# Decode attention from 64 KiB rows: four heads in a tile, three slots, K transposed in place

## The chip, the cores and the metric

The kernel runs on one core of one Trainium2 chip. The metric is the device time in microseconds (us) of one execution, the median of several.

## The reference

One decode step: layer norm, attention over a cache of 8192 keys for 4 sequences and 32 heads, and a gated feed-forward part (FFN), added to x.

```python
q = (xn @ wq).reshape(4, 1, 32, 128).transpose(0, 2, 1, 3)
scores = einsum("bhqd,bhkd->bhqk", q, k_cache) * 128 ** -0.5   # k_cache: 4 x 32 x 8192 x 128, bf16
o = einsum("bhqk,bhkd->bhqd", softmax(scores), v_cache)
return x + o.reshape(4, 1, 4096) @ wo + (silu(xn @ w_gate) * (xn @ w_up)) @ w_down
```

K and V are 268 MB each, and every byte is read once. That makes this a kernel of transfers: 551 MB in all.

## The kernel before

A tile is one sequence and HT = 2 heads of K or of V: 4 MiB, 32 KiB of contiguous memory for each of the 128 partitions (64 partitions a head, 128 keys each). Five slots of 32 KiB per partition hold what is loaded. VectorE turns K in blocks of 32 x 32 (r = QB = 32 in the access pattern), piece by piece into buffers of its own; TensorE makes scores from these; P V of tile i - 2 follows.

```python
HT = 2; T = HT * Sk // P          # 128 keys a partition
SLOT = T * Dh; NSLOT = 5; LP = 2
slots = tc.tile_pool(name="slots", bufs=NSLOT)
kt_pool = tc.tile_pool(name="ktp", bufs=5)
def load_k(n):
    j, b = divmod(n, B)
    t_ = slot()
    nc.sync.dma_start(out=t_[:], in_=A_k_cache[b, j * HT:(j + 1) * HT, :, :]
                      .rearrange("h (p t) d -> (h p) (t d)", t=T))
def t_piece(n, g):                # 16 keys of every partition
    kt = kt_pool.tile([P, w], dt.bfloat16, name="kt")
    nc.vector.transpose(out=kt[:]..., in_=k_tiles[n][:, g * w:(g + 1) * w]...)
for i in range(NT + LP):
    load_k(i + 2); load_v(i)
    for g in range(NTG):
        t_piece(i, g); s_piece(i, g)        # transpose, then 4 score matmuls
    # ... maximum and exponentials of two tiles at once, P V of tile i - 2 ...
```

Of the kernel before, what the change touches and what calls it, by code (L numbers as in the profile page):

```python
# [8 lines left out]
dt = mybir.dt  # L9
# [6 lines left out]
def kernel(  # L16
# [20 lines left out]
    assert D % P == 0 and F % P == 0 and Sk == 64 * P and H % 4 == 0  # L37
# [3 lines left out]
    HT = 2  # L41
# [8 lines left out]
    NSLOT = 5  # L50
    LP = 2
# [13 lines left out]
    kt_pool = ctx.enter_context(tc.tile_pool(name="ktp", bufs=5))  # L65
    pp = ctx.enter_context(tc.tile_pool(name="pp", bufs=2))
# [18 lines left out]
    x_sb = persist.tile([B, D], dt.bfloat16, name="x_sb")  # L85
    nc.scalar.dma_start(out=x_sb[:], in_=x_flat[:, :])
    wq_t = slot()
    nc.sync.dma_start(out=wq_t[:], in_=A_wq.rearrange("(p c) n -> p (c n)", c=EC))
# [9 lines left out]
    def load_v(n, parts=(T,)):  # L98
        j, b = divmod(n, B)
        t_ = slot()  # L100
        src = A_v_cache[b, j * HT:(j + 1) * HT, :, :].rearrange("h (p t) d -> (h p) (t d)", t=T)
        c0 = 0
        for w in parts:
            c1 = c0 + w * Dh
            nc.sync.dma_start(out=t_[:, c0:c1], in_=src[:, c0:c1])
            c0 = c1
        v_tiles[n] = t_
# [5 lines left out]
    ident = const.tile([P, P], dt.bfloat16, name="ident")  # L113
    make_identity(nc, ident[:])
# [4 lines left out]
    zq = [const.tile([P, 2, 4, ZW], dt.bfloat16, name=f"zq{i}") for i in range(2)]  # L119
    for z_ in zq:  # L120
        nc.gpsimd.memset(z_[:], 0.0)
# [8 lines left out]
    def by_row(ap):  # L130
        return ap.rearrange("p (y a b g r) -> p y b a g r", y=HT, a=2, b=2, r=2)[:, :, :, :, :, 0]

    rowb = const.tile([P, HT, 2], dt.float32, name="rowb")
    nc.vector.reduce_sum(out=rowb[:], in_=by_row(ident_f[:]), axis=AX.XY)
    rowb_q = const.tile([P, HT, 2], dt.float32, name="rowb_q")
# [12 lines left out]
    xf = persist.tile([B, D], dt.float32, name="xf")  # L148
    nc.vector.tensor_copy(out=xf[:], in_=x_sb[:])
    xsum = persist.tile([B, 1], dt.float32, name="xsum")  # L150
    nc.vector.reduce_sum(out=xsum[:], in_=xf[:], axis=AX.X)
    mean = persist.tile([B, 1], dt.float32, name="mean")
    nc.vector.tensor_scalar(out=mean[:], in0=xsum[:], scalar1=1.0 / D, scalar2=None, op0=ALU.mult)
    xc = kt_pool.tile([B, D], dt.float32, name="kt")
    nc.vector.tensor_scalar(out=xc[:], in0=xf[:], scalar1=mean[:, 0:1], scalar2=None, op0=ALU.subtract)
    sq = kt_pool.tile([B, D], dt.float32, name="kt")
    nc.vector.tensor_tensor(out=sq[:], in0=xc[:], in1=xc[:], op=ALU.mult)
    vsum = persist.tile([B, 1], dt.float32, name="vsum")
    nc.vector.reduce_sum(out=vsum[:], in_=sq[:], axis=AX.X)
# [4 lines left out]
    xn_bf = kt_pool.tile([B, D], dt.bfloat16, name="kt")  # L164
    nc.vector.tensor_scalar(out=xn_bf[:], in0=xc[:], scalar1=rstd[:, 0:1], scalar2=None, op0=ALU.mult)  # L165
# [16 lines left out]
    q_bf = slots.tile([P, NH, 2, 8, NQ, QB], dt.bfloat16, name="slot")  # L182
# [10 lines left out]
    pick = ident[:].rearrange("p (c x) -> p c x", c=NQ)[:, :, 0:B]  # L193
# [8 lines left out]
    yfx = persist.tile([B, D], dt.float32, name="yfx")  # L202
    otn = persist.tile([P, H, B], dt.bfloat16, name="otn")

    DH = D // 2
    yo_ps = [psY.tile([B, DH], dt.float32, name="yo_ps") for _ in range(2)]
    ffn = {}

    def load_ffn():
        wgu_t, wd_t = slot(), slot()  # L210
        w = EC * F
        nc.sync.dma_start(out=wgu_t[:, 0:w], in_=B_w_gate.rearrange("(p c) f -> p (c f)", c=EC))
        nc.sync.dma_start(out=wgu_t[:, w:2 * w], in_=B_w_up.rearrange("(p c) f -> p (c f)", c=EC))
        nc.sync.dma_start(out=wd_t[:, 0:FC * D], in_=B_w_down.rearrange("(p c) e -> p (c e)", c=FC))
        ffn["w"] = (wgu_t[:, 0:w].rearrange("p (c f) -> p c f", c=EC),
                    wgu_t[:, w:2 * w].rearrange("p (c f) -> p c f", c=EC),
                    wd_t[:, 0:FC * D].rearrange("p (c e) -> p c e", c=FC))

    def do_ffn():
        wg, wu, wd = ffn["w"]  # L220

        gu_ps = psM.tile([P, 2, FC * B], dt.float32, name="mps")
        for i, w in enumerate((wg, wu)):
            for fc in range(FC):
                for c in range(EC):
                    mm(gu_ps[:, i, fc * B:(fc + 1) * B], w[:, c, fc:F:FC], xnt_w[:, c, 0:B],
                       start=(i == 0 and fc == 0 and c == 0))
        eg = persist.tile([P, FC * B], dt.float32, name="eg")
        nc.scalar.activation(out=eg[:], in_=gu_ps[:, 0, :], func=ACT.Exp, scale=-1.0)
        nc.vector.tensor_scalar(out=eg[:], in0=eg[:], scalar1=1.0, scalar2=None, op0=ALU.add)  # L230
        sig = persist.tile([P, FC * B], dt.float32, name="sig")
        nc.vector.reciprocal(out=sig[:], in_=eg[:])
        gs = persist.tile([P, FC * B], dt.float32, name="gs")
        nc.vector.tensor_tensor(out=gs[:], in0=gu_ps[:, 0, :], in1=sig[:], op=ALU.mult)
        ht = persist.tile([P, FC * B], dt.bfloat16, name="ht")
        nc.vector.tensor_tensor(out=ht[:], in0=gs[:], in1=gu_ps[:, 1, :], op=ALU.mult)
        yf_ps = psM.tile([B, D], dt.float32, name="mps")
        for fc in range(FC):
            mm(yf_ps[0:B, :], ht[:, fc * B:(fc + 1) * B], wd[:, fc, :], start=(fc == 0))
        nc.vector.tensor_tensor(out=yfx[:], in0=yf_ps[0:B, :], in1=xf[:], op=ALU.add)  # L240

        for j in range(2):
            mm(yo_ps[j][0:B, :], ident_f[0:B, 0:B], yfx[:, j * DH:(j + 1) * DH], start=True)
# [6 lines left out]
    def load_wo():  # L250
        t_ = slot()
# [8 lines left out]
    kts, s_ps, pt, nmx, osb, rcp = {}, {}, {}, {}, {}, {}  # L260
    rs_t = {}

    def build_q(gr):
        j, bp = divmod(gr, 2)
        for a in range(NQ):
            h = j * HT + a // 2
            half, cg, hh = h // 16, (h % 16) // 4, h % 4
            nc.vector.tensor_copy(  # L268
                out=zq[gr % 2][a * QB:(a + 1) * QB, :, :, XO + a * QB].rearrange("p b (j r) -> p r j b", r=2),
                in_=qt[a * QB:(a + 1) * QB, half, :, hh * 2:hh * 2 + 2, cg * B + bp * 2:cg * B + bp * 2 + 2])  # L270

    def t_piece(n, g):

        w = TG * Dh
        kt = kt_pool.tile([P, w], dt.bfloat16, name="kt")
        src = k_tiles[n][:, g * w:(g + 1) * w].bitcast(dt.uint32)
        nc.vector.transpose(out=kt[:].bitcast(dt.uint32).rearrange("p (j t r) -> p t j r", j=2, r=QB),  # L277
                            in_=src.rearrange("p (t j r) -> p t j r", j=2, r=QB))
        kts[n, g] = kt

    def s_piece(n, g):
        gr, bb = divmod(n, 2)
        if bb == 0 and g == 0:
            s_ps[gr] = psS.tile([P, 512], dt.float32, name="sps")
        kt = kts.pop((n, g))[:].rearrange("p (j n r) -> p j n r", j=2, r=2)
        off = XO - 2 * (bb * NTG + g)
        for jp in range(4):
            mm(s_ps[gr][:], zq[gr % 2][:, bb, jp, off:off + P], kt[:, jp // 2, :, jp % 2],
               start=(bb == 0 and g == 0 and jp == 0))

    def max_1(gr):
        mx = small.tile([P, 1], dt.float32, name="mx")
        nc.vector.reduce_max(out=mx[:], in_=s_ps[gr][:], axis=AX.X)  # L293
        nmx[gr] = mx

    def max_2(gr):

        mps = psM.tile([P, 512], dt.float32, name="mps")
        nc.tensor.matmul(mps[:, 0:P], lhsT=nmx.pop(gr)[:, 0:1].to_broadcast([P, P]), rhs=ident_f[:, :],  # L299
                         is_transpose=True, start=True, stop=True, skip_group_check=True)  # L300
        nm = small.tile([P, HT, 2], dt.float32, name="nm")
        nc.vector.tensor_reduce(out=nm[:], in_=by_row(mps[:, 0:P]), axis=AX.XY, op=ALU.max, negate=True)  # L302
        nc.vector.tensor_tensor(out=nm[:], in0=nm[:], in1=rowb_q[:], op=ALU.mult)
        nb = small.tile([P, 1], dt.float32, name="nb")
        nc.vector.reduce_sum(out=nb[:], in_=nm[:], axis=AX.XY)
        p_ = pp.tile([P, 512], dt.bfloat16, name="p_")
        rs = small.tile([P, 1], dt.float32, name="rs")
        nc.scalar.activation(out=p_[:], in_=s_ps.pop(gr)[:], func=ACT.Exp, bias=nb[:, 0:1], scale=qscale,
                             accum_out=rs[:])
        pt[gr] = p_  # L310
        rs_t[gr] = (rs, mps)

    def pt_turn(gr):
        p_ = pt[gr]
        t_ = ptz[gr % 2]
        HP = P // HT
        for y in range(HT):
            nc.vector.transpose(out=t_[y * HP:(y + 1) * HP, :, y, :, :].rearrange("p s u x -> p s (u x)"),  # L318
                                in_=p_[y * HP:(y + 1) * HP, :].rearrange("p (s w) -> p s w", s=4))
        pt[gr] = t_[:].rearrange("p s y u x -> p (s y u x)")  # L320

    def row_sums(gr):
        j, bp = divmod(gr, 2)
        rs, mps = rs_t.pop(gr)
        mm(mps[:, P:P + B], rs[:, 0:1].to_broadcast([P, P]), rowb[:].rearrange("p y b -> p (y b)"), start=True)
        if bp == 0:
            rcp[j] = small.tile([P, HT, B], dt.float32, name="rcp")
        nc.vector.reciprocal(out=rcp[j][:, :, 2 * bp:2 * bp + 2],  # L328
                             in_=mps[:, P:P + B].rearrange("p (y b) -> p y b", y=HT))

    def p_off(n, k):
        g, s = divmod(k, TG // NV)
        return s * HT * NV * QB + 2 * ((n % 2) * NTG + g)

    def pv_chunk(n, k):
        j, b = divmod(n, B)
        w = HT * NV
        off = p_off(n, k)
# [151 lines left out]
```

## Time and profile before

| | before |
|---|---|
| time, median of 3 | 1288.92 us (1288.82 to 1288.93) |
| DMA main queue, share of 16 engines' span | 99.4% |
| DMA packets | 21529, 551.49 MB |
| PE / VectorE busy | 84% / 57% |
| instructions | 11189 |

Read the transfers first. When 16 engines are full from the first to the last slice, the busy shares of PE and VectorE say only how much room they have. The lines are in the prediction below. A "packet" is one record of a DMA transfer in the trace. Here that is one partition's row: the trace has 16256 packets of 32 KiB, as many as 127 tiles of 128 rows.

### The profile page before, as it was taken

What the parts mean: (1) busy time and instruction counts of PE and PEld (TensorE: products, weight loads), DVE (VectorE), ACT (ScalarE), POOL (GpSimd) and SP (SyncE); (2) the same over time, 40 slices, a digit from 0 to 9 for tenths busy, and PEclk for the clock granted to TensorE, in tenths of its full rate; (3) what the DMA queues carried; (4) which work ended last, traced back from release to release, by engine and by line L of the source; (5) the groups of instructions that cost most, each with busy time, mean ns of one, the idle gap of its engine ahead of it and who ended that gap; (6) DMA issues with size and microseconds to landing.
All of it is one profiled execution on the core that took longest, in us unless ns stands there. A gap on an engine that the chain in (4) does not pass through costs nothing.

```text
span 1287.1 us, 11189 instructions
## 1 busy us (share of the span) xinstructions
PE 1083.1 (84%) x4778; PEld 430.3 (33%) x4778; DVE 738.1 (57%) x951; ACT 39.7 (3%) x87; POOL 5.3 (0%) x13
## 2 busy tenths in 40 slices
PE   4888888888888798897997888888887988978788
PEld 1334333333333333332333333333333333333334
DVE  6663556546556556466556566465465465573544
ACT  1000000000000000000000000000000000000000
POOL 1000000000000000000000000000000000000000
PEclk9898898998989999898998989989899898989899
DMA  9999999999999999999999999999999999999997
GB/s 407 427 430 435 437 425 437 429 436 431 432 435 428 436 432 433 431 432 435 431 435 428 434 432 431 436 431 433 430 434 431 437 430 432 433 431 427 433 434 304
DMA packets 21529, 551.49 MB, mean 428 GB/s; under 512 B 2268, under 2 KB 2792, under 8 KB 3944
## 3 DMA queue, kind: packets, MB, share of 16 engines
q1 hardware_dynamic: 21464, 550.78, 99.4%
q8 instruction: 37, 0.61, 0.2%
q14 instruction: 12, 0.10, 0.0%
q10 hardware_dynamic: 16, 0.01, 0.0%
HBM read 550.77 MB, written 0.00 MB: 428 GB/s over the span
## 4 chain that ended last, share of the span: by engine, by line
DMA 50%; PE 31%; DVE 14%; issue 5%; ACT 1%; SPq 0%; DVEq 0%
DMA slot<-in_A_k_cache_dram 44%; PE oacc L76 17%; PE sps L76 12%; DVE kt L277 11%; DMA slot<-in_A_v_cache_dram 6%; PE mps L76 1%; DVE ptz L318 1%; DVE o L356 1%; PE xps L76 1%; DVE o_sb L354 1%; ACT o_sb L353 0%; PE mps L299 0%; DVE otn L377 0%; PE yo_ps L76 0%; DVE rcp L328 0%
## 5 line engine op out<-in xcount | busy, mean ns | idle before, releaser
L76 PE MATMUL sps<-kt,zq 128*128 128x512 bf16 x2048 | 578.3, 421 | 145.2 <-DVE kt L277 128.7
L277 DVE STREAM_TRANSPOSE kt<-slot 128x1024 uint32<-128x1024 uint32 x512 | 587.6, 1210 | 90.4 <-DMA slot<-in_A_k_cache_dram 89.5
L76 PE MATMUL oacc<-slot,ptz 128*8 128x512 bf16 x2016 | 450.4, 379 | 0.4 <-DMA slot<-in_A_v_cache_dram 0.4
L76 PEld LDWEIGHTS <-zq 128*128 128x128 bf16 x2048 | 212.0, 104 | 496.1 <-issue 317.0
L76 PEld LDWEIGHTS <-ptz 128*8 128x8 bf16 x2016 | 177.5, 92 | 258.1 <-issue 27.8
L328 DVE RECIPROCAL rcp<-mps 128x4 f32<-128x4 f32 x32 | 5.9, 183 | 281.9 <-PE mps L76 281.9
L354 DVE TENSOR_TENSOR o_sb<-o_sb,rowu 128x512 f32<-128x512 f32 x16 | 11.1, 693 | 89.2 <-ACT o_sb L353 89.0
L76 PE MATMUL xps<-rowy,o 128*32 128x4 f32 (+1 forms) x228 | 13.5, 205 | 37.3 <-DVE o L356 37.3
L293 DVE TENSOR_REDUCE mx<-sps 128x1 f32<-128x512 f32 x32 | 22.1, 692 | 18.5 <-PE sps L76 18.5
L76 PEld LDWEIGHTS xps<-rowy,o 128*32 128x32 f32 (+1 forms) x228 | 12.1, 154 | 44.9 <-DVE o L356 44.9
L268 DVE COPY zq<-qt 32x8 bf16<-32x8 bf16 x128 | 21.3, 166 | 1.3
L302 DVE TENSOR_REDUCE nm<-mps 128x4 f32<-128x64 f32 x32 | 7.2, 225 | 24.0 <-PE mps L299 24.0
L356 DVE TENSOR_REDUCE o<-o_sb 128x128 f32<-128x512 f32 x16 | 16.3, 1020 | 0.5
L76 PEld LDWEIGHTS mps<-rowb,rs 128*128 128x128 f32 x64 | 9.5, 186 | 13.8 <-issue 13.8
L76 PEld LDWEIGHTS <-slot 128*128 128x128 bf16 x272 | 11.7, 126 | 3.5 <-DVE slot L188 2.6
L76 PE MATMUL mps<-rowb,rs 128*128 128x4 f32 x64 | 12.3, 263 | 0.0
L353 ACT COPY o_sb<-oacc 128x512 f32<-128x512 f32 x16 | 9.4, 586 | 76.8 <-PE oacc L76 76.8
L377 DVE TENSOR_TENSOR otn<-xps,rcp 32x16 bf16<-32x16 f32 x28 | 4.8, 170 | 11.7 <-PE xps L76 10.3
L299 PE MATMUL mps<-ident_f,mx 128*128 128x128 f32 x32 | 10.3, 323 | 0.8 <-DVE mx L293 0.8
L299 PEld LDWEIGHTS mps<-ident_f,mx 128*128 128x128 f32 x32 | 4.3, 133 | 14.7 <-DVE mx L293 14.2
L170 PE MATMUL xps<-ident,kt 4*128 4x4 bf16 x4 | 0.3, 173 | 10.1 <-DVE kt L165 10.1
L76 PE MATMUL yo_ps<-slot,otn 128*4 128x256 bf16 x64 | 8.2, 281 | 0.3 <-DVE otn L366 0.3
(150 smaller groups left out, 148.5 us busy)
## 6 DMA issues: line engine op xcount, KB each, us to landing
slot<-in_A_k_cache_dram SPq DMA_DIRECT2D x64, 4096.0 KB, 39.2
slot<-in_A_v_cache_dram SPq DMA_DIRECT2D x62, 4096.0 KB, 36.8
slot<-in_A_v_cache_dram SPq DMA_DIRECT2D x7, 1024.0 KB, 22.3
slot<-in_A_wq_dram SPq DMA_DIRECT2D x1, 4096.0 KB, 12.3
slot<-in_A_wo_dram SPq DMA_DIRECT2D x1, 3584.0 KB, 40.2
slot<-in_B_w_gate_dram SPq DMA_DIRECT2D x1, 1792.0 KB, 31.9
slot<-in_B_w_up_dram SPq DMA_DIRECT2D x1, 1792.0 KB, 35.8
slot<-in_B_w_down_dram SPq DMA_DIRECT2D x1, 1792.0 KB, 30.9
```

The costliest lines, as they stand in the source:

```text
L76: nc.tensor.matmul(out_ap, lhsT=lhsT, rhs=rhs, start=start, stop=True, skip_group_check=True, **kw)
L268: nc.vector.tensor_copy(out=zq[gr % 2][a * QB:(a + 1) * QB, :, :, XO + a * QB].rearrange("p b (j r) -> p r j b", r=2), in_=qt[a * QB:(a + ...
L277: nc.vector.transpose(out=kt[:].bitcast(dt.uint32).rearrange("p (j t r) -> p t j r", j=2, r=QB), in_=src.rearrange("p (t j r) -> p t j r", ...
L293: nc.vector.reduce_max(out=mx[:], in_=s_ps[gr][:], axis=AX.X)
L299: nc.tensor.matmul(mps[:, 0:P], lhsT=nmx.pop(gr)[:, 0:1].to_broadcast([P, P]), rhs=ident_f[:, :], is_transpose=True, start=True, stop=True ...
L302: nc.vector.tensor_reduce(out=nm[:], in_=by_row(mps[:, 0:P]), axis=AX.XY, op=ALU.max, negate=True)
L318: nc.vector.transpose(out=t_[y * HP:(y + 1) * HP, :, y, :, :].rearrange("p s u x -> p s (u x)"), in_=p_[y * HP:(y + 1) * HP, :].rearrange( ...
L328: nc.vector.reciprocal(out=rcp[j][:, :, 2 * bp:2 * bp + 2], in_=mps[:, P:P + B].rearrange("p (y b) -> p y b", y=HT))
L353: nc.scalar.copy(out=o_sb[:].rearrange("p u d -> p (u d)"), in_=o_acc[j % 2][:])
L354: nc.vector.tensor_tensor(out=o_sb[:], in0=o_sb[:], in1=rowu[:].unsqueeze(2).to_broadcast([P, NV, Dh]), op=ALU.mult)
L356: nc.vector.reduce_sum(out=o1[:], in_=o_sb[:].rearrange("p u d -> p d u"), axis=AX.X)
L377: nc.vector.tensor_tensor(out=otn[q0:q1, blk * 4:blk * 4 + 4, :], in0=xps[q0:q1], in1=r_[q0:q1, y, :].unsqueeze(1).to_broadcast([QB, 4, B] ...
```

## The change

The intent is longer rows, so fewer packets. With HT = 4 a tile is 8 MiB and a row 64 KiB. The kernel keeps three such slots (192 KiB a partition, for 160 KiB in five before) and little else of size beside them: K is transposed in place in its slot, V(i) is loaded into the slot that K(i) has left, small things of the start lie beside wq, and P V of a tile is cut into halves that lie on both sides of the next tile's scores.

```diff
-    HT = 2
+    HT = 4
-    NSLOT = 5
-    LP = 2
+    NSLOT = 3
-    kt_pool = ctx.enter_context(tc.tile_pool(name="ktp", bufs=5))
-    def t_piece(n, g):
-        kt = kt_pool.tile([P, w], dt.bfloat16, name="kt")
-        nc.vector.transpose(out=kt[:]..., in_=src...)
+    def turn_k(n, parts):
+        t0 = 0
+        for w in parts:
+            t1 = t0 + w * TG
+            ap = k_tiles[n][:, t0 * Dh:t1 * Dh].bitcast(dt.uint32)
+            nc.vector.transpose(out=ap, in_=ap)
+            t0 = t1
+    for i in range(NT - 1):
+        turn_k(i, (2,) * 8 if i < 2 else (4, 4, 2, 2, 2, 2))
+        if i >= 3:
+            pv_to(i - 2, NK)            # second half of P V(i - 2)
+            load_k(i + 1)
+        for g in range(NTG):
+            score(i, g)
+        ...  load_v(i)                  # into the slot of K(i)
+        max_1(i)
+        pv_to(i - 1, 8); max_2(i); pt_turn(i)
+        pv_to(i - 1, NK // 2)           # first half of P V(i - 1)
+        row_sums(i)
+    # the last tile: wo with half of V, the other half in pieces of 48, 32, 24, 16 and 8 keys
```

(Cut: the end, the FFN in one slot with its sum straight into the output's PSUM, the finish of a group of heads in PSUM without ScalarE's copy.)

## The prediction

> **What bounds the kernel now.** I read the page from the top. The first view is the span in slices and the DMA totals.
>
> ```profile
> span 1287.1 us, 11189 instructions
> PE 1083.1 (84%) x4778; PEld 430.3 (33%) x4778; DVE 738.1 (57%) x951; ACT 39.7 (3%) x87; POOL 5.3 (0%) x13
> DMA  9999999999999999999999999999999999999997
> GB/s 407 427 430 435 437 425 437 429 436 431 432 435 428 436 432 433 431 432 435 431 435 428 434 432 431 436 431 433 430 434 431 437 430 432 433 431 427 433 434 304
> DMA packets 21529, 551.49 MB, mean 428 GB/s; under 512 B 2268, under 2 KB 2792, under 8 KB 3944
> q1 hardware_dynamic: 21464, 550.78, 99.4%
> ```
>
> The 16 DMA engines are busy in every slice but the last, and the main queue alone fills 99.4% of the span. PE at 84% and VectorE (DVE) at 57% have room. The windows view says how the edges differ from the middle; its last two columns are the DMA share and GB/s.
>
> ```profile
> 0.00:2.00 2.00, 0.00 (x0) 0.00 (x0) 1.03 (x4) 0.67 (x1) 1.33 (x9) 1.00 0.64 166
> 640.00:960.00 320.00, 272.29 (x1140) 106.20 (x1137) 189.69 (x241) 8.57 (x20) 0.00 (x0) 0.94 1.00 432
> 1270.00:1280.00 10.00, 10.00 (x108) 5.24 (x106) 1.40 (x3) 0.59 (x1) 0.00 (x0) 1.00 0.78 327
> 1280.00:1287.00 7.00, 3.35 (x74) 2.42 (x70) 1.09 (x3) 0.36 (x1) 0.00 (x0) 0.59 0.11 44
> ```
>
> So the time is: about 1.8 us of start, a transfer that never pauses, and a tail. Last comes the chain at the end, in order of time (start, length, what):
>
> ```profile
> 1265.54 17.13 DMA slot<-in_A_v_cache_dram
> 1282.67 0.05 issue
> 1282.71 0.60 PE xps L76 x16
> 1283.32 0.03 issue
> 1283.34 0.18 DVE otn L366
> 1283.52 0.04 issue
> 1283.56 1.03 PE yo_ps L76 x4
> 1284.59 0.02 issue
> 1284.61 0.36 ACT res L458
> ```
>
> The last piece of V lands at 1282.7, and 4.4 us of work and output follow. The page's chain of waits puts only 50% on DMA, which would mislead: it steps through what released each DMA issue, though another transfer was still moving at that moment. The slices decide.
>
> I then took the trace's records of single DMA packets. In the median a packet of 1024, 4096, 8192, 14336 and 32768 B takes 46, 159, 309, 535 and 1213 ns. The slope from 4096 to 32768 B is 1054 ns per 28672 B, 36.76 ns per 1000 B or 27.2 GB/s an engine; what is left over is 1213 - 1204.6 = 8.4 ns a packet, whatever its size. A 4-byte packet (a completion) takes 9 ns. All packet times sum to 1281.5 us for each of 16 engines. At nearly every moment 16 data packets are in flight; only from about 1275 on are there 9, for some 4 us, as seven engines have finished first.
>
> [...] 432 GB/s in the middle, 27.2 x 16 = 435 from the slope. [...] the trace shows 8.4, so I use 8.4.[...] eight pieces of 1024 uint32 took 9.11 us, 1.14 us each, so about 1.11 ns an element with its start.
>
> **The change, part by part.**
>
> *Longer rows.* HT = 4 makes a K or V tile 8 MiB with 64 KiB per partition. Before, 127 tiles (wq, 64 K, 62 V) of 128 rows give 16256 packets of 32 KiB; that is the count in the trace. After, 32 K and 30 V tiles give 62 x 128 = 7936 rows of 64 KiB. If each is one packet, it should take 65536 B x 36.76 = 2409.4, plus 8.4, so 2418 ns against 2 x 1213 = 2426. Work per engine: 7936 x 2418 / 16 = 1199.3 us; wq 128 x 1213 / 16 = 9.7; the 31st V in four parts of 16 KiB rows, 512 x 611 / 16 = 19.6; the last V's first half 256 x 611 / 16 = 9.8; its pieces of 48, 32, 24, 16 and 8 keys, 128 x (460 + 309 + 234 + 159 + 84) / 16 = 10.0; wo 8.9 + 1.5; FFN weights 384 x 535 / 16 = 12.8; instruction fetches as before, 37 x 929 / 16 = 2.1. Completions: some 81 transfers for 141, x 16 x 9 ns / 16 = 0.7 for 1.3. Sum 1274.4. The same sum for before, with its median packet times, is 1279.3, and the records have 1281.5 as some packets are slower; so add 2.2: **1276.6 against 1281.5, a gain of 4.9 us**. The bytes themselves do not change.
>
> *Three slots instead of five.* This is the risk: does a transfer ever have to wait for a slot? An 8 MiB tile takes 8.39 MB / 0.432 = 19.4 us, so a round (one K, one V) is 38.8 us. Let K(i) land at 0. V(i-1) then moves until 19.4, K(i+1) until 38.8, and V(i) must be ready to issue by 38.8 into K(i)'s own slot. VectorE turns K(i) from 0: 16384 elements a partition in six instructions, at 1.14 us per 1024 at most (18.2 us). PE first does the second half of P V(i-2), 32 x 0.22 = 7 us (the trace: 32 in 7.08), which frees the slot for K(i+1) at about 1 to 8, due at 19.4: 11 us or more in hand. The scores follow the transposes and end some 2.5 us after the last, at about 21; V(i) is due at 38.8: **18 us in hand**. PE per round: 64 scores paced by VectorE (18 to 20 us), 64 P V x 0.22 = 14.2, small things about 1: some 34 of 38.8. VectorE per round: 18.2, maximum and its three small ones 1.3, four turns of P about 2.5, row sums, q and the finish about 1.5: 24 of 38.8. Neither becomes the bound.
>
> *The start.* wq lands at 12.3, K0 about 32, K1 about 51. V0 goes into wq's slot, free near 20, due at 51. The FFN weights go into K0's slot after scores 0 (32 + 18 + 3 = 53, due at 70); K2 into K1's slot after scores 1 (near 77, due at 83, the tightest); V1 after all of P V(0) (near 93, due at 102); K3 after the FFN (near 104, due at 121). Estimates, each with 6 us or more.
>
> *The end.* K31, V30, wo with half of V31, then the other half into K31's slot: scores 31 end some 20 us after K31 lands, and V30 and the wo load (38 us) run meanwhile. After the last landing come 8 small matmuls for 16 (0.3 for 0.6 us), the same scaling (0.2), four heads x 4 matmuls of 128 columns for two heads x 2 of 256 (about 1.2 for 1.0), and the output. The tail stays near 4.4 us; sum of this part 0.
>
> *In place on VectorE, ScalarE's copy dropped.* 512 transposes become about 200[...], all beside the transfers: worth 0.
>
> Sum: 1288.9 - 4.9 = **1284.0 us**.
>
> **Rivals.**
> 1. *A wait for a slot takes the place of what is won.* For it: three slots, K(i) and V(i) sharing one, and a load of 8 MiB lands only as a whole. Against it: 18 us in hand. If transposing in place were half as slow again (27 us), scores would end at 30, still in time; twice as slow (36), they would end at 38.8, and each round loses a few us: 31 rounds x 2 us = 60, or 1345. A wait in the start alone costs 5 to 10 us: 1290 to 1294.
> 2. *A 64 KiB row goes as two packets of 32 KiB.* Nothing in this trace tells. Then only the completions are saved: 1288.
> 3. *HBM dislikes the 64 KiB pitch.*[...] A loss of 1 to 3% would make 1297 to 1325.
> 4. *A gain over 2%* needs 1263 us[...].
>
> **Range and chances.** The centre is 1284, with rival 2 (about one in four) at 1288, so 1279 to 1293 should hold it 8 times in 10. Under 1279 only if the slower packets of before go too. Faster by over 2%: 0.01. Slower by over 2% (over 1314.7), from rival 1 or 3 in full: 0.05. Within 2%: 0.94.
>
> **What would show it.** Right: a DMA line of nines with 432 to 436 GB/s throughout, some 13,000 packets in all, the 64 KiB packets at about 2418 ns, their sum near 1277, DMA issues of V(i) well before the transfer ahead ends, and an end like that of before. Two packets a row: 21,000 packets again. Wrong by rival 1: slices under 425 GB/s in the middle, and K landing later than 38.8 us after the last. Wrong by rival 3: engines busy all through at a lower GB/s, packets over 2418. The mean of a transpose should be near 2.3 us for 2048 elements; over 4 us would mean that in place is slow.

The places marked as cut in the prediction held figures and reasons that no trace or run of this case shows. Rival 3 stays as a possibility that had not been measured, with an assumed loss; against rival 4, the trace's slope gives an estimate: 551.5 MB at 27.2 x 16 = 435 GB/s take 1267 us, more than the 1263 it needs. Times of the kernel after with "about" or "some" are estimates from the trace of the kernel before. One of them is the 1.2 us for 16 matmuls of 128 columns at the end: the trace of the kernel before has 16 of 256 columns in 1.91 us, and 1.03 was measured after. That an 8 MiB load is of use only as a whole (rival 1) is how the kernel after ran: while K(i+1) was moving, from 668 to 687.0 us, VectorE stood idle for its last 10.8 us.

## The result

The changed kernel took **1285.91 us** (median of 4, 1285.87 to 1285.94) against 1288.87 us for the kernel before in the same session: 2.96 us less. The ratio is 0.9977 with an interval of 0.9962 to 0.9992. The forecast was 1284.0 and 4.9 us less, range 1279 to 1293.

The page of the kernel after, its span, engines, DMA and queue lines:

```profile
span 1284.1 us, 11309 instructions
PE 1003.1 (78%) x5170; PEld 460.9 (36%) x5170; DVE 736.5 (57%) x621; ACT 30.1 (2%) x71; POOL 5.9 (0%) x12
DMA  9999999999999999999999999999999999999997
GB/s 425 423 432 430 443 429 431 432 437 427 438 437 431 433 431 441 427 425 448 431 425 444 434 423 439 439 425 433 439 431 429 435 433 438 429 433 442 427 414 313
DMA packets 12600, 551.49 MB, mean 429 GB/s; under 512 B 1277, under 2 KB 1801, under 8 KB 3081
q1 hardware_dynamic: 12536, 550.77, 99.2%
```

The line of nines is the same as before, the bytes are the same, and the packets have gone from 21529 to 12600. A row of 64 KiB did go as one packet: the trace has 7936 of 65536 B. (Single slices now swing between 414 and 448 GB/s, so the prediction's sign "432 to 436 throughout" does not hold slice by slice, and some slices in the middle lie under its warning mark of 425. The time did not follow, and the windows view below is level. The swing goes with the size of the packets: slices 2 to 38 lie between 423 and 448 here, between 425 and 437 with 32 KiB rows, before, and between 429 and 432 with 16 KiB rows, in a_quarter below.) The windows view of the kernel after, as in the prediction (busy by engine, PE clock, DMA share, GB/s):

```profile
640.00:960.00 320.00, 253.72 (x1134) 112.81 (x1133) 181.72 (x149) 6.22 (x16) 0.00 (x0) 0.90 1.00 434
1270.00:1280.00 10.00, 6.29 (x194) 5.85 (x192) 0.00 (x0) 0.00 (x0) 0.00 (x0) 0.50 0.58 239
```

In the middle 434 GB/s stand against 432 before, and the end is of the same kind. The chain of waits at the end of the kernel after (start, length, what):

```profile
1255.84 23.23 DMA slot<-in_A_v_cache_dram
1279.07 0.05 issue
1279.11 0.59 PE xps L74 x16
1279.70 0.03 issue
1279.73 0.39 PE xps L74 x8
1280.12 0.02 issue
1280.15 0.18 DVE otn L380
1280.33 0.04 issue
1280.38 1.03 PE yo_ps L74 x16
1281.41 0.02 issue
1281.43 0.26 ACT res L486
```

V's second last piece lands at 1279.1 and its last about 0.6 us later, against 1282.7 before, and the rest takes as long as it did, 4.4 us. So the gain lies before the last landing, in the stream of transfers.

How the three slots behave shows in the timeline of VectorE in one round (start, length, what, in brackets the idle time before it):

```profile
648.39 17.54 DVE L298 STREAM_TRANSPOSE slot<-slot 128x4096 uint32<-128x4096 uint32 x6 [10.50 <-DMA slot<-in_A_k_cache_dram]
668.32 0.69 DVE L311 TENSOR_REDUCE mx<-sps 128x1 f32<-128x512 f32 x1 [2.39 <-PE sps L74]
...
671.95 2.85 DVE L335 STREAM_TRANSPOSE ptz<-p__3063 32x512 bf16<-32x512 bf16 x4 [0.93 <-ACT p__3063 L326]
676.02 0.18 DVE L345 RECIPROCAL rcp<-mps 128x4 f32<-128x4 f32 x1 [1.22 <-PE mps L74]
686.98 4.45 DVE L298 STREAM_TRANSPOSE slot<-slot 128x4096 uint32<-128x4096 uint32 x1 [10.77 <-DMA slot<-in_A_k_cache_dram]
```

K lands at 648.4 and the next K at 687.0, 38.6 us apart, the time that two tiles of 8.39 MB take at 434 GB/s. VectorE is done with everything by 676.2 and waits for K: it is the transfers that set the round. In the same round K(i+1) was issued at 644.7 and V(i) at 668.3 (the timeline of all engines):

```profile
644.72 0.33 SPq L104 DMA_DIRECT2D slot<-in_A_k_cache_dram  x1
668.31 0.33 SPq L117 DMA_DIRECT2D slot<-in_A_v_cache_dram  x1
```

**Where the 3 us are.** I took the records of single packets of both traces. The 64 KiB packet takes 2418 ns, as forecast. All packet times sum to 1277.1 us an engine, on average over the 16, against 1281.5: 4.5 us less, close to the forecast 4.9. But the last landing came only 3.0 us earlier. The length of a packet is not the distance to the next one: the commonest distance from a packet's start to the start of the one that follows is 2414 ns at 64 KiB and 1209 to 1210 ns at 32 KiB, so 3.5 to 4 ns of each packet lie under the next. Where a completion (4 bytes) comes between, the distance is 2420, and 1215 to 1216: 6 ns for a completion, not 9. Two rows of 32 KiB against one of 64: 2 x 1209.5 - 2414 = 5 ns; less rounding, 4.7 ns for each packet saved (1209.4 less the 1204.7 that 32 KiB take at the slope). Saved are 496 packets and 62 completions an engine: 496 x 4.7 + 62 x 6 ns = 2.7 us. That was the theory to test.

### The profile page after: what moved, and what is told of

It reads as the page before. It is cut to its first block, busy times and chain, and to the rows that moved or that the text cites. A ratio compares the mean times of both kernels' runs of the same rounds, so it can differ in the third digit from the quotient of the medians.

```text
span 1284.1 us, 11309 instructions
## 1 busy us (share of the span) xinstructions
PE 1003.1 (78%) x5170; PEld 460.9 (36%) x5170; DVE 736.5 (57%) x621; ACT 30.1 (2%) x71; POOL 5.9 (0%) x12
## 2 busy tenths in 40 slices
DMA packets 12600, 551.49 MB, mean 429 GB/s; under 512 B 1277, under 2 KB 1801, under 8 KB 3081
## 4 chain that ended last, share of the span: by engine, by line
DMA 53%; PE 35%; DVE 9%; SPq 2%; issue 0%; ACT 0%; DVEq 0%; ACTq 0%
DMA slot<-in_A_k_cache_dram 48%; PE sps L74 18%; PE oacc L74 16%; DVE slot L298 8%; DMA slot<-in_A_v_cache_dram 5%; SPq L117 1%; SPq L275 1%; PE mps L74 1%; DVE ptz L335 1%; PE yo_ps L74 0%; PE mps L317 0%; PE xps L74 0%; DVE oacc L368 0%; DVE o L370 0%; ACT p__1242 L326 0%
## 5 line engine op out<-in xcount | busy, mean ns | idle before, releaser
L298 DVE STREAM_TRANSPOSE slot<-slot 128x2048 uint32<-128x2048 uint32 (+1 forms) x198 | 561.8, 2901 | 294.7 <-DMA slot<-in_A_k_cache_dram 294.7
L74 PE MATMUL sps<-slot,zq 128*128 128x512 bf16 x2048 | 516.0, 415 | 246.5 <-DVE slot L298 246.4
L74 PE MATMUL oacc<-slot,ptz 128*16 128x512 bf16 x1920 | 430.8, 380 | 0.4 <-DMA slot<-in_A_v_cache_dram 0.4
L74 PEld LDWEIGHTS <-ptz 128*16 128x16 bf16 x1920 | 195.1, 106 | 209.4 <-issue 13.1
L74 PEld LDWEIGHTS <-slot 128*128 128x128 bf16 (+2 forms) x716 | 25.7, 110 | 20.6 <-DMA slot<-in_A_v_cache_dram 7.8
L74 PE MATMUL xps<-ptz,slot 128*128 128x4 bf16 x512 | 15.3, 169 | 7.3 <-DMA slot<-in_A_v_cache_dram 7.2
L288 DVE COPY zq<-qt 32x8 bf16<-32x8 bf16 x64 | 11.1, 174 | 0.7
L74 PE MATMUL yo_ps<-slot 128*4 128x128 bf16 (+1 forms) x60 | 3.6, 308 | 8.4 <-DVE yo_ps L167 6.8
L74 PE MATMUL yo_ps<-slot,otn 128*4 128x128 bf16 x128 | 6.4, 288 | 3.7 <-DMA slot<-in_A_wo_dram 3.5
L74 PEld LDWEIGHTS <-otn 128*4 128x4 bf16 x128 | 6.0, 115 | 3.9 <-issue 3.5
```

Of the source, the lines that this page charges most:

```text
L74: nc.tensor.matmul(out_ap, lhsT=lhsT, rhs=rhs, start=start, stop=True, skip_group_check=True, **kw)
L288: nc.vector.tensor_copy(out=zq[a * QB:(a + 1) * QB, :, :, XO + a * QB].rearrange("p b (j r) -> p r j b", r=2), in_=qt[a * QB:(a + 1) * QB, ...
L298: nc.vector.transpose(out=ap, in_=ap)
```

## The experiments

Each run's edit is against the kernel after if not said otherwise. Beside each the kernel before ran on the same chip: 1289.00, 1288.97 and 1289.06 us median. The kernel after ran again (after_again, at the end); the runs are set against its time there or in the result, as the kernel before shows the three to be alike within 0.1 us.

### Rows cut again: packets, transfers, or something else

**a_half.** Every whole tile comes as two transfers of 32 KiB rows. Packets and completions are then about those of the kernel before, with everything else of the change kept.

```diff
-        nc.sync.dma_start(out=t_[:], in_=src)
+        for c in range(2):
+            w = SLOT // 2
+            nc.sync.dma_start(out=t_[:, c * w:(c + 1) * w], in_=src[:, c * w:(c + 1) * w])
-    def load_v(n, parts=(T,)):
+    def load_v(n, parts=(T // 2,) * 2):
```

> The kernel after, but every whole K and V tile (32 K, 30 V) comes as two transfers of 32 KiB rows, as many K and V packets as in the kernel before; slots, rounds, start and end as after. Theory A (the gain is the packets saved, at the cost that the starts of following packets show: 2414 ns from start to start at 64 KiB against 2 x 1209.5 at 32 KiB, so 4.7 ns a packet, and 6 ns a completion): 62 x 8 = 496 packets and 62 completions more per engine, +2.3 + 0.4 = +2.7 us, 1288.6. Theory A with the 8.4 ns of the prediction: +4.2 + 0.6 = +4.7 us, 1290.6. Theory B (the gain is of the slots, the start or the end, not of the packets): 1285.9, unchanged.

Measured: 1288.34 us. **a_quarter** cuts into four in the same way.

> The kernel after with every whole tile as four transfers of 16 KiB rows: 1488 packets and 186 completions more per engine. Theory A at 4.7 and 6 ns: +7.0 + 1.1 = +8.1 us, 1294.0. At 8.4 and 9 ns: +12.5 + 1.7 = +14.2 us, 1300.1. Theory B: 1285.9.

Measured: 1294.45 us. Both are near the first number (4.7 ns a packet) and far from the second (8.4 ns) and from no change. The last landing of V in the profiled executions says the same: 2.6 us later than in the kernel after for a_half, 8.1 us for a_quarter. The page's DMA lines of a_half, then of a_quarter:

```profile
DMA packets 21528, 551.50 MB, mean 429 GB/s; under 512 B 2268, under 2 KB 2792, under 8 KB 4072
```

```profile
DMA packets 39385, 551.52 MB, mean 427 GB/s; under 512 B 4252, under 2 KB 4776, under 8 KB 6056
```

**a_one** tells packets from transfers. One transfer fills a row from two places 4 MiB apart, so rows of K and V mix heads and the result is wrong.

```diff
+        src = A_k_cache[b, j * HT:(j + 1) * HT, :, :].rearrange("h s d -> (h s d)")
+        nc.sync.dma_start(out=t_[:].rearrange("p (x f) -> p x f", x=2),
+                          in_=src.rearrange("(x p f) -> p x f", x=2, p=P))     # V likewise
```

> Wrong results on purpose: the kernel after, but in 60 of the whole loads (K 0 to 31 and V 0 to 29, 62 in all) one transfer fills each row from two places 4 MiB apart, so that its packets are 32 KiB while the number of transfers and completions is that of after. Against the run with two transfers a tile it tells packets from transfers. Theory A at 4.7 ns a packet: 496 packets more, +2.3 us, 1288.2, that is 0.4 under the run with two transfers. Theory C (the cost is by transfer, its issue and completion, not by packet): 1285.9. At 8.4 ns: 1290.1.

(All 62 whole loads were changed; the "60" there is a slip.) Measured: 1288.22 us, with 20535 packets but only the small ones of the kernel after, which had 1277:

```profile
DMA packets 20535, 551.49 MB, mean 429 GB/s; under 512 B 1276, under 2 KB 1800, under 8 KB 3080
```

The cost is by packet: 2.3 us come with the packets alone (1288.22 - 1285.90, the yardstick measured below), 4.7 ns for each of the 496. What the second transfer of each tile adds is small and not settled: 0.1 us between the medians, with ranges that touch (1288.04 to 1288.34 and 1288.32 to 1288.61), and 0.5 us between the last landings of V in the two profiled executions, where 0.4 was expected. The comparison with the reference at its tolerance doesn't see mixed heads.

**b_half** is the kernel before with the same cut, 16 KiB rows in five slots (its edit has the same form and is left out here).

> The kernel before with its 64 K tiles and the 62 whole V tiles as two transfers of 16 KiB rows each: 126 x 8 = 1008 packets and 126 completions more per engine, with five slots. Theory A at 4.7 and 6 ns: +4.7 + 0.8 = +5.5 us, 1294.4. At 8.4 and 9 ns: +8.5 + 1.1 = +9.6 us, 1298.5. Theory B: the kernel before is not paced by packets, 1288.9.

Measured: 1295.47 us, 6.5 us over the kernel before, where 5.5 was expected. The chain of waits at the end of b_half:

```profile
1271.09 17.19 DMA slot<-in_A_v_cache_dram
1288.28 0.05 issue
```

The last V lands at 1288.28, 5.6 us later than in the kernel before, as the packet count would have it. The rest came after it. In the packet records one of the eight output rows of 512 B comes behind an 8 KiB instruction fetch and goes at 1292.07, about 0.6 us after the others (that it waited for the fetch is inferred). So the packet cost is the same with five slots of 4 MiB (5.6 us for 1008 packets and 126 completions an engine) as with three of 8 MiB (5.5 us between the last landings of a_half and a_quarter, for 992 and 124).

### How much room the three slots leave

**t_13** makes VectorE's work in a round longer. A transpose done three times gives the same result.

```diff
             nc.vector.transpose(out=ap, in_=ap)
+            if t0 >= 10 * TG and n < NT - 1:
+                nc.vector.transpose(out=ap, in_=ap)
+                nc.vector.transpose(out=ap, in_=ap)
```

> The kernel after, but the last three transposes of each K tile (six of its sixteen pieces) are done three times, which leaves the same result, so that VectorE and the end of the scores come 3 x 2 x 2.27 = 13.6 us later in each round. VectorE: 23 + 13.6 = 36.6 us of a 38.8 us round. Slack theory (V(i) is issued 18 us before the transfer ahead of it ends): still hidden, 1286 to 1287. Rival 1 of the prediction (the slots already pace the rounds): about 31 x 13.6 us more, 1700.

Measured: **1470.13 us**. Both expectations missed. Its DMA lines show holes:

```profile
DMA  9939989988888989888988889988889888889877
GB/s 426 408 133 417 423 375 395 427 361 355 373 371 371 427 357 384 371 359 388 398 373 371 372 345 427 398 370 368 350 371 428 371 372 366 375 373 427 371 331 330
```

**t_18** does the same with the first eight pieces (`t0 < 8 * TG`).

> The kernel after with the first eight pieces of each K tile turned three times: 4 x 4.42 = 17.7 us more VectorE a round (a little more in the first two). VectorE: 23 + 17.7 = 40.7 us, over the round of 38.8. Slack theory: VectorE now sets the round, some 30 x 1.9 = 57 us less a few us of slack used up once: 1325 to 1350, and the DMA shows holes. Rival 1: 1285.9 + 31 x 17.7 = 1835.

Measured: **1577.39 us**, again between the two. The fault was mine in the theory: I had taken VectorE's busy time (23 us a round) as what it needs. In the timeline of the kernel after it does the work of a round in the order of the program, and between waits for the scores (2.39 us), for P V before the maximum's matmul (1.41), for the exponentials (0.93) and for the row sums (1.22). This makes 648.4 to 676.2 = 28 us a round, not 23. With 13.6 us more that is 42, over 38.8; t_13 indeed runs at 43 to 44 us a round. (In the round from 665.5 to 708.7 the repeats took 14.1 us and the waits had grown by 1.2 us.) VectorE begins the next K right after the row sums (the timeline of t_13):

```profile
708.47 0.18 DVE L348 RECIPROCAL rcp<-mps 128x4 f32<-128x4 f32 x1 [1.22 <-PE mps L74]
708.68 13.16 DVE L298 STREAM_TRANSPOSE slot<-slot 128x4096 uint32<-128x4096 uint32 x4
```

No idle time for K is left there (11.3 us in the whole of t_13, for 294.7 in the kernel after), so VectorE with its waits sets the round. In the start t_13 also opened one hole of 27 us near 83 us, where K2 waits for the slot of K1. **t_9** tests the new reading with 8.9 us more in K 2 to 30 (`t0 < 4 * TG and 2 <= n < NT - 1`).

> The kernel after with the first transpose (four of sixteen pieces) of K 2 to 30 done three times: 2 x 4.46 = 8.9 us more VectorE a round. The run with 13.6 us more fell to 44 us a round. New theory (VectorE does its work in program order, and a round of it with its waits for scores, maximum, exponentials and row sums is 28 us long, from 648.4 to 676.2 in the profile after, and some 2 us more where a group of heads is finished, so 9 to 11 of 38.8 us are free, which is also its mean wait for K, 294.7 / 31 = 9.5 us): 8.9 us just fit, 1286 to 1288, no holes. Rival 1 (slots pace the rounds, no slack): +29 x 8.9 = 258 us. If the slack of a round were only some 5 us: +110 us.

Measured: 1285.94 us, no change. So the free time of a round is 8.9 us or more and under 13.6. The waits view says the same in one line, of the kernel after and then of t_9 (waited for K, us in total, times, longest):

```profile
DVE slot L298 <- DMA slot<-in_A_k_cache_dram: 294.7, 31, 11.8
```

```profile
DVE slot L298 <- DMA slot<-in_A_k_cache_dram: 39.9, 24, 11.4
```

The first is 9.5 us a round, all that was free; the repeats of t_9 used up nearly all of it.

**p_front** takes the halves of P V away: all 64 matmuls of tile i - 1 go ahead of the next scores.

```diff
-            pv_to(i - 1, 8)
+            pv_to(i - 1, 8 if i in (1, NT - 2) else 0)
-            pv_to(i - 1, NK if i in (1, NT - 2) else NK // 2)
+            pv_to(i - 1, NK if i in (1, NT - 2) else 0)
```

> The kernel after without its halves of P V around the scores: all 64 matmuls of P V(i-1) go ahead of the scores of the next tile (in the two rounds where they were not halved they stay). K(i+1) is then issued some 7 us later, still due 19 us after K(i) lands, and scores end at about 2.4 us after the last transpose as before. Theory (P V's order is off the path): 1285.9, within 0.5. Rival (the halves are what keeps the third slot free in time): each round loses some us, over 1300.

Measured: 1285.85 us, no change. The halves are not what makes three slots work; the order of P V has room.

### What else is in the time of both kernels

**m_more** adds 64 small matmuls (32 columns, into an unused part of a PSUM tile) to each of 31 rounds.

```diff
+        mps_x = rs_t[i][1]
+        for _ in range(64):
+            mm(mps_x[0:QB, 256:256 + QB], xnt_w[:, 0, :], xnt_w[:, 0, :], start=True)
         row_sums(i)
```

> The kernel after with 64 small matmuls more in each of 31 rounds (1984, that is 3968 instructions more for PE, some 4 us of PE a round, which has the room). In the traces 16 KiB instruction fetches, one in every 32 us, come in a pattern that repeats after eight, and eight or nine of the DMA engines fall behind the others through the whole run, 7.5 us at the end. Theory (fetches of instructions make these engines late and the last transfer waits for them): 15 fetches more, 2 for each of eight engines at 7.5 us / 5 = 1.5 us each, +3 us, 1288.9, and the spread of the engines at the end grows to about 10 us. Rival (only the bytes count, 0.25 MB over 16 engines): +0.6 us, spread unchanged.

Measured: 1288.76 us, 2.85 us more. The queue line of instruction fetches, of the kernel after and then of m_more (packets, MB, share):

```profile
q8 instruction: 40, 0.66, 0.2%
```

```profile
q8 instruction: 56, 0.92, 0.3%
```

(The 15 fetches expected were an estimate; at 40 for the 11309 instructions of the kernel after, 3968 more would bring 14.) Sixteen fetches more, and the spread of the 16 engines at the last landing of V, read from the completions in the trace, grew from 7.5 to 10.4 us. It is a real part of both kernels: before it was 7.8 us, and in both traces seven engines are done while eight or nine still move the last V. The packets of the last V tell the fetches from a general delay: the seven early engines end at 1272.2 to 1272.8 us in the kernel after and at 1272.2 to 1272.9 in m_more, the latest at 1279.7 and 1282.6. And the spread grows in steps through the whole kernel after, about 1.4 us for every eight fetches: 1.9 us at 182, 3.3 at 377, 4.7 at 687, 6.2 at 1114, 7.5 at the end. That eight of the engines carry the fetches is inferred: the lengths of the fetches repeat after eight. The trace does not name the engine of a packet. At 2.85 us for 16 fetches the 40 of the kernel after would be some 7 us (an estimate).

**best** uses this: P V of the tile before last in 64 wide matmuls instead of 256 narrow ones, and some rows near the end in fewer packets (three lines that follow from these are cut from the edit below). **after_again** is the unchanged yardstick.

```diff
-            pv_still(n - 1, xps, (g - 7) // 2 * 32, (g - 5) // 2 * 32, start=(g == 7))
+            pv_to(n - 1, (g - 5) // 2 * 8)
-            load_v(i, (T // 4,) * 4)
+            load_v(i, (T // 2,) * 2)
-    v_from(n, t_, H * D, 0, (T // 4, T // 4))
+    v_from(n, t_, H * D, 0, (T // 2,))
```

> A version meant to beat both: the kernel after with P V of the tile before last in 64 matmuls of 512 columns instead of 256 of 4 (192 pairs of weight load and matmul fewer; the run with 1984 pairs more had 16 more instruction fetches and took 2.85 us more, so 1.5 fetches fewer, -0.28 us), and with that V in two transfers for four and the first half of the last V in one for two (24 packets and 3 completions fewer per engine, -0.13 us). Theory: -0.4 us against the kernel after in the same call, about 1285.5. Rival (the end is set by the last landing alone and these do not reach it): the same as after.

> The kernel after, unchanged, as the yardstick for the others of this call: 1285.9, within 0.2.

Measured: best 1285.73 us (1285.67 to 1286.38, 4 runs), after_again 1285.90 us (1285.88 to 1285.97, 6 runs). The medians differ by 0.17 us where 0.4 was expected, and their ranges overlap: no gain is shown. It had 12166 packets and 39 fetches for 40.

## Why the prediction was right, and where a term was off

- **The bound and the verdict** were right: transfers all through, no gain over 2% and no loss. The forecast gain of 4.9 us was measured as 3.0.
- **The row as one packet** (rival 2 fell): 7936 packets of 64 KiB at 2418 ns, 12600 packets in all, packet times summing to 1277.1 for 1276.6 forecast.
- **The mis-sized term was "8.4 ns a packet" and 9 ns a completion.** That is how much longer a packet's record is than its bytes, but records overlap. From start to start a packet costs 4.7 ns and a completion about 6. Three sizes agree: 607 ns from start to start at 16 KiB in a_quarter and b_half, 1209 to 1210 at 32 KiB, 2414 at 64 KiB, each 4.5 to 5 ns over the slope. In place of 4.9 us this gives 2.7 us. The direct test, a_half against after, gives 2.4 us (1288.34 - 1285.91).
- **What is left over.** a_half has the packets and completions of before and is still 0.7 us faster (1288.34 to 1289.00). The runs of before spread by 0.9 us, but the two ranges do not overlap (at most 1288.61, at least 1288.73). The holes at the end, where fewer than 16 data packets are in flight, are worth 3.8 us of all engines before, 3.4 after and 3.3 in a_half, so half a microsecond may lie there. (The prediction kept 37 instruction fetches; the kernel after has 40, but the spread of the engines at the end did not grow by it.) No run tests this; it stays open.
- **The end** stayed as it was, as forecast. **The start** too: the FFN weights, K2, V1 and K3 were issued at 51.9, 77.3, 91.6 and 103.8 us for 53, 77, 93 and 104 forecast.
- **Three slots** (rival 1): in the change as it is, V(i) was issued 18.7 us before K(i+1) had landed, "18 us in hand" as said, and slots cost nothing. Half as slow again would still fit, it said, and t_9, with 8.9 us more, did. But the rival's size was wrong. It said that transposing twice as slowly would end in time for V and lose about 2 us a round. t_18, which turns K in 35 us, lost (1577 - 1286) / 30 = 9.7 us a round, its holes in the start included. The step that failed is "VectorE per round: 24 of 38.8": it summed busy time and left out the waits in order, which make it 28, and so 9.5 us of room on average where 15 seemed to be. That the slots held all the same is owed to that remaining room, not to this sum.
- **In place:** 2270 ns for 2048 elements and 4424 for 4096, the size forecast; no loss from it shows. The transposes of K took 26 us less of VectorE (561.8 for 587.6), but its total fell only from 738.1 to 736.5 us, as other work grew: turning P takes 2.85 us a tile now, and took 1.38 us for two tiles, as much work, before. None of it shows in the time, as the transfers set it.
- **HBM pitch** (rival 3 fell): 64 KiB rows ran at 434 GB/s from 640 to 960 us, against 432 before, and a_one, with two places 4 MiB apart in a row, at 433. (No trace had shown a loss from a pitch.)

## What to carry to other kernels

Where transfers fill the span, write the time as bytes over the rate, plus packets times their cost, plus the two ends, and take the cost of a packet from start to start, not from the length of its record (here 4.7 ns, not 8.4). With rows of 32 to 64 KiB little was left in that term: halving 64 KiB rows cost 2.4 us of 1286 (a_half), and halving again 6.1 us (a_quarter). When slots or buffers get fewer, count the room of an in-order engine by its whole round with its waits, because that, not its busy time, is where the next change will strike: here 28 us, not 23, so that 8.9 us more still fitted into 38.8 (t_9) and 13.6 did not (t_13).
